# First expert on inputs without their norm in every block, and the second expert's weight words converted in place

## The chip, the cores and the metric

One core of a Trainium2 chip. The metric is the device time of one execution, in microseconds (us). TensorE does the matrix products, VectorE, ScalarE and GpSimd (POOL in the rows) the elementwise work, SyncE issues the DMAs.

## The reference

Attention of 4 batches, 8 heads, 576 positions, head size 64: heads 0 to 3 see the last 32 positions, heads 4 to 7 every 32nd position. Its output, 2304 tokens by 512, goes through two experts in series, each 512 to 1536 to 512:

```python
x = attention(q, k, v)                                    # 2304 x 512
xn = x / sqrt(mean(x * x, axis=-1) + 1e-6) * rms_g
x2 = (silu(xn @ w_gate) * (xn @ w_val)) @ w_out           # expert 1
out = (x2 @ w_a * (x2 @ w_b)) @ w_out2                    # expert 2
```

The norm of a token is one factor for its whole row. So `xn @ w` is `(x * rms_g) @ w` times that factor, and the value product's factor may be put on expert 1's output.

## The kernel before

**Tiling.** The tokens are cut into 6 blocks of 384 (96 positions of each of the 4 batches; columns of a tile), d_ff into 12 slots of 128. Expert 1 runs block after block: per slot 12 matmuls of the gate product (`g_ps`), 12 of the value product (`v_ps`) and 12 of the output `y` of the slot before. Each product is three matmuls of split numbers (high by high, high by low, low by high, `mm3`, L474 to L477), so its input `xx` is a pair: a high half, cast on ScalarE, and a low half, the difference, on VectorE or GpSimd. `h = sg * v_ps` (L747) is split in the same way into `hl` (L489 cast on ScalarE, L490 difference).

**PSUM.** `g_ps` and `v_ps` take turns in three banks, so a bank is used again 36 matmuls after its product is complete; `y` has four banks, and one bank, `att`, is left to the attention.

**Attention beside it.** While block t goes through the expert, the attention of block t+1 is put into its slots (`attention_slot`, L600; the string table `LOCAL`, L51 to L54, says which step stands in which slot). Local heads run on TensorE with softmax on VectorE and ScalarE (`s_t`, L298 to L332). Strided heads are products on GpSimd (`prod`, L232 and L265) and sums on VectorE (`S_t` L235, `xs_t` L268), 57 of each. Every instruction's place on its engine is then set by a scheduler, so the order on an engine differs from the order of the code.

**The norm before.** Blocks 1 to 5: the attention's output is copied out of PSUM (`x_t`, L381 and L397, ScalarE), squared (`sq`) and summed with one matmul (`rms`), the square root goes to ScalarE and the reciprocal to VectorE (`rinv`, L427). Then `xprep` (L430) makes for each of the 4 channel tiles `xn = x_t * g * rinv` on VectorE (L433), the high half `xx` (L437, ScalarE) and the low half (L438: VectorE for blocks 2 and 4, GpSimd for 1, 3 and 5, by the string `XLO`). These steps stand in slot 11 of the block before, and the block's first matmul needs the first of them. Block 0 does it in another way: `xx` is made from the output times `g` alone, each gate product is multiplied by the reciprocal `ri0` on VectorE (L736) ahead of Silu (L737), and so is each of the four `y` (L588).

**Outputs.** The four `y` of a block are taken out of PSUM in slot 1 of the next block (`evac_y`: `ys` on ScalarE, L590, for blocks 1 to 5) and written to DRAM (`x2d`).

**Block 5.** It has no attention beside it. Instead the second expert's weights are turned into seven sums per group, the forms (`convert_forms`, L622): a raw tile (`raw`, 2 buffers, load L106), its words (`words`: a Prelu on ScalarE, L129, writes the tile `cy`, one buffer; a second ScalarE pass, L134, writes `z0` or `z1`, one buffer each; VectorE puts the two together in `z`, L137), casts on ScalarE (L142), differences (L143) and sums (`zs`, L656 to L659, on GpSimd where the group's number is odd, else on VectorE). Also `slab` tiles of block 0's and 1's output are loaded and subtracted (L693). Loads stand in SyncE's one queue in order. From 593.7 us on only the second expert runs.

## Time and profile before

| | |
|---|---|
| median of 3 runs | 1018.35 us (1016.94 to 1019.04) |
| the profiled execution | 1017.75 us, its span 1016.0 us |
| mean granted clock of TensorE | 0.973 |
| first gate matmul of blocks 1 to 5 | 141.5, 228.8, 317.2, 406.1, 501.9 us |
| expert 1 ends | 593.7 us |

Times in the rows are microseconds from the span's start, means are nanoseconds. A busy time counts instructions in work, not in wait. In the waits, the line left of the arrow waited and the one at its right came last. The granted clock of a stretch is a mean: 1.00 is 2.4 GHz, and a part of it at 1.2 GHz counts one half.

### The profile page before, as it was taken

The numbers are of one execution on the slowest core, as the hardware profiler recorded it, in microseconds if no ns is written. First come the engines' busy times: TensorE is split into PE (matmuls) and PEld (weight loads), VectorE is DVE, ScalarE is ACT, GpSimd is POOL, SyncE is SP. The second block draws the span as 40 slices with busy tenths as digits, with TensorE's granted clock in tenths as the row PEclk, the third lists the DMA queues.
The fourth block names the chain that finished last, engine by engine and source line by source line (L and its number), as shares of the span: only waits on it lengthen the run. The fifth ranks groups of instructions, "written<-read, shape, count | busy, mean of one in ns | idle before, by whom it ended". The sixth has DMA issues, their size and how long they took to land.

```text
span 1016.0 us, 14355 instructions
## 1 busy us (share of the span) xinstructions
PE 961.8 (95%) x5438; PEld 908.7 (89%) x5438; DVE 640.6 (63%) x869; ACT 427.5 (42%) x832; POOL 543.2 (53%) x416
## 2 busy tenths in 40 slices
PE   6898799999999999699959999999999999999998
PEld 5698699998998999599959999999999998999996
DVE  5699957538808674978366536866856556455444
ACT  4878645236223523342366552644533432222110
POOL 4588747456729776678365722656651533223111
PEclk6999999999999999899989999999999999999999
DMA  9953357435534453242299946599894783772701
GB/s 349 407 208 122 107 188 279 130 115 171 165 113 151 154 173 122 88 142 81 90 341 367 372 156 252 197 392 394 311 376 190 286 301 136 272 308 105 271 40 63
DMA packets 57365, 215.57 MB, mean 212 GB/s; under 512 B 5968, under 2 KB 14544, under 8 KB 51664
## 3 DMA queue, kind: packets, MB, share of 16 engines
q1 hardware_dynamic: 57296, 214.66, 58.0%
q8 instruction: 43, 0.70, 0.3%
q14 instruction: 26, 0.21, 0.1%
HBM read 172.17 MB, written 42.47 MB: 211 GB/s over the span
## 4 chain that ended last, share of the span: by engine, by line
PE 69%; DVE 13%; ACT 6%; POOL 4%; issue 4%; DMA 3%; SPq 0%; DVEq 0%; POOLq 0%; ACTq 0%
PE o L878 4%; PE o L880 4%; PE o L879 4%; PE Y L822 3%; PE Y L824 3%; PE Y L823 3%; PE g_ps L476 3%; PE v_ps L475 3%; PE v_ps L476 3%; PE g_ps L475 3%; PE y L476 3%; PE v_ps L477 3%; PE g_ps L477 3%; PE y L475 3%; PE y L477 3%
## 5 line engine op out<-in xcount | busy, mean ns | idle before, releaser
L143 POOL TENSOR_TENSOR hl<-c,hl 128x384 fp32r<-128x384 f32 x72 | 77.4, 1076 | 190.8 <-ACT hl L142 180.2
L232 POOL TENSOR_TENSOR prod<-kv_t,qs_t 128x512 f32<-128x512 f32 (+12 forms) x57 | 106.8, 1894 | 18.9 <-DVE S_t L235 6.1
L475 PE MATMUL g_ps<-xx,gv 128*128 128x384 f32 x288 | 100.6, 349 | 12.7 <-DVE h L747 11.4
L490 POOL TENSOR_TENSOR hl<-h,hl 128x384 fp32r<-128x384 f32 x58 | 63.6, 1096 | 79.4 <-ACT hl L489 78.0
L475 PE MATMUL v_ps<-xx,gv 128*128 128x384 f32 x288 | 98.6, 343 | 7.2 <-ACT sg L737 4.8
L476 PE MATMUL g_ps<-xx,gv 128*128 128x384 f32 x288 | 100.4, 349 | 4.9 <-DVE xx L438 4.9
L477 PE MATMUL g_ps<-xx,gv 128*128 128x384 f32 x288 | 99.6, 346 | 0.0
L477 PE MATMUL y<-hl,wo 128*128 128x384 f32 x288 | 99.0, 344 | 0.0
L829 DVE TENSOR_TENSOR c<-c,Y 128x384 f32<-128x384 f32 x108 | 59.1, 551 | 63.2 <-PE Y L824 57.8
L476 PE MATMUL y<-hl,wo 128*128 128x384 f32 x288 | 98.3, 341 | 0.3 <-DVE hl L490 0.2
L265 POOL TENSOR_TENSOR prod<-kv_t,S_t 128x512 f32<-128x512 f32 (+12 forms) x57 | 85.4, 1511 | 23.8 <-issue 7.8
L476 PE MATMUL v_ps<-xx,gv 128*128 128x384 f32 x288 | 98.0, 340 | 0.0
L477 PE MATMUL v_ps<-xx,gv 128*128 128x384 f32 x288 | 97.6, 339 | 0.0
L268 DVE TENSOR_REDUCE xs_t<-prod 128x64 f32<-128x448 f32 (+17 forms) x57 | 85.4, 1517 | 13.2 <-POOL prod L265 13.0
L747 DVE TENSOR_TENSOR h<-sg,v_ps 128x384 f32<-128x384 f32 x72 | 39.0, 542 | 80.7 <-PE v_ps L477 62.3
L475 PE MATMUL y<-hl,wo 128*128 128x384 f32 x288 | 85.4, 344 | 0.6 <-ACT hl L489 0.6
L878 PE MATMUL o<-slab,hl 128*128 128x512 f32 x216 | 84.6, 392 | 1.0 <-DVE slab L887 0.5
L879 PE MATMUL o<-slab,hl 128*128 128x512 f32 x216 | 84.6, 392 | 0.0
L880 PE MATMUL o<-slab,hl 128*128 128x512 f32 x216 | 83.4, 394 | 0.0
L142 ACT CAST hl<-c 128x384 fp32r<-128x384 f32 x72 | 36.9, 513 | 109.5 <-DVE c L859 109.3
L822 PE MATMUL Y<-slab,form 128*128 128x384 f32 x216 | 73.1, 338 | 0.1
L824 PE MATMUL Y<-slab,form 128*128 128x384 f32 x216 | 73.1, 338 | 0.0
(142 smaller groups left out, 2546.5 us busy)
## 6 DMA issues: line engine op xcount, KB each, us to landing
form<-formd SPq DMA_DIRECT2D x32, 1792.0 KB, 10.6
wo<-wod SPq DMA_DIRECT2D x60, 512.0 KB, 3.7
raw<-in_w SPq DMA_DIRECT2D x42, 512.0 KB, 5.5
gv_raw<-in_w SPq DMA_DIRECT2D x30, 512.0 KB, 10.1
formd<-form SPq DMA_DIRECT2D x6, 1792.0 KB, 9.1
formd<-forms SPq DMA_DIRECT2D x6, 1792.0 KB, 11.1
slab<-x2d SPq DMA_DIRECT2D x24, 384.0 KB, 5.8
wod<-wo SPq DMA_DIRECT2D x12, 512.0 KB, 2.9
```

The costliest lines, as they stand in the source:

```text
L143: lo_eng.tensor_tensor(lo, x, hi.bitcast(F32), op=ALU.subtract)
L232: nc.gpsimd.tensor_tensor(pr, st["ks", g][:, :, :n, :], st["qs"][:, heads(g), mm:mm + 1, :].to_broadcast([128, G, n, D]), op=ALU.mult)
L265: st["pvm"] = nc.gpsimd.tensor_tensor(pr, st["vs", g][:, :, :n, :], st["S"][:, heads(g), mm, :n, None].to_broadcast([128, G, n, D]), op=AL ...
L268: st["pvr"] = nc.vector.tensor_reduce(st["xs"][:, mm, heads(g), :], pr.rearrange("p g n d -> p g d n"), axis=X, op=ALU.add)
L475: nc.tensor.matmul(out_ps, w_hi, x_hi, start=start, stop=False)
L476: nc.tensor.matmul(out_ps, w_hi, x_lo, start=False, stop=False)
L477: nc.tensor.matmul(out_ps, w_lo, x_hi, start=False, stop=stop)
L822: nc.tensor.matmul(bank(n), hi, x[p][:, 0, c], start=begins and c == 0, stop=False, skip_group_check=not begins)
L824: nc.tensor.matmul(bank(n), lo, x[p][:, 0, c], start=False, stop=c == 1, skip_group_check=not begins)
L878: nc.tensor.matmul(o, h[:, 0, cols], w[0], start=n == 0, stop=False)
L879: nc.tensor.matmul(o, h[:, 0, cols], w[1], start=False, stop=False)
L880: nc.tensor.matmul(o, h[:, 1, cols], w[0], start=False, stop=n == len(chunks) - 1)
```

## The change

Blocks 1 to 5 are done as block 0. As soon as an attention output stands in PSUM, `xsplit` takes it out times `g` (`x_t`, ScalarE), squares it from PSUM, and makes both halves of `xx` (the low one on the engine that `XLO` says). `xprep` with its 20 `xn` on VectorE is gone. All 60 gate products of blocks 1 to 5 are multiplied by `ri[t]` on VectorE, Silu then reads that tile, and the 20 `ys` of blocks 1 to 5 go from ScalarE's copies to VectorE's products. The forms' words have no `cy` any more: Prelu writes into the odd words of the raw tile itself, so the raw tile is in use until VectorE has put the words together. The same holds for the second expert's output weights (the last part of the diff). Instructions: VectorE 871 before, 931 after; ScalarE 782 and 764; TensorE, GpSimd and SyncE keep their numbers.

```diff
-          "lnorm0 lvl0 pt0 ptc0 lnorm1 lvl1|pt1 ptc1 lnorm2 pt2 ptc2||pv0 pvc0 pv1 pvc1 sq0|sq1|"),
+          "lnorm0 lvl0 pt0 ptc0 lnorm1 lvl1|pt1 ptc1 lnorm2 pt2 ptc2||pv0 pvc0 pv1 pvc1||"),
...
-          "lnorm0 lexp1 lvl1 pt0 ptc0 lnorm1 lnorm2|pt1 pt2 ptc1||ptc2 pv0 pvc0 pv1 pvc1 sq0 sq1||")]
+          "lnorm0 lexp1 lvl1 pt0 ptc0 lnorm1 lnorm2|pt1 pt2 ptc1||ptc2 pv0 pvc0 pv1 pvc1||")]
...
-            st["y"] = pool.tile([128, DM], F32, tag="cy", name="cy", bufs=ncy)
+            st["y"] = pool.tile([128, DM], F32, tag="cy", name="cy", bufs=ncy) if ncy else raw[:, :, 1].bitcast(F32)
...
+        def xsplit(i, src):
+            x_t = piece("xr", "x_t", 4)
+            nc.scalar.activation(x_t, src, AF.Copy, scale=g_sb[:, i:i + 1])
+            sq(i)()
+            xx = xt[t, i] = act.tile([128, 2, NTB], F32R, tag="x", name="xx", bufs=8)
+            nc.scalar.copy(xx[:, 0], x_t)
+            engine(XLO[t]).tensor_tensor(xx[:, 1], x_t, xx[:, 0].bitcast(F32), op=ALU.subtract)
...
-                x_t = st["x", p] = piece("xr", "x_t", 4)
-                nc.scalar.copy(x_t, st["ops", p][:, :NTB])
+                xsplit(p, st["ops", p][:, :NTB])
...
-                src = st["ops" if i < 2 else "xps", i % 2][:, :NTB] if t == 0 else st["x", i]
+                src = st["ops" if i < 2 else "xps", i % 2][:, :NTB]
...
-        def xprep(cc):
-            def f():
-                xn = act.tile([128, NTB], F32, tag="t", name="xn", bufs=NTMP)
-                nc.vector.scalar_tensor_tensor(
-                    xn, st["x", cc],
-                    g_sb[:, cc:cc + 1], st["ri"], op0=ALU.mult, op1=ALU.mult)
-                xx = act.tile([128, 2, NTB], F32R, tag="x", name="xx", bufs=8)
-                nc.scalar.copy(xx[:, 0], xn)
-                engine(XLO[t]).tensor_tensor(xx[:, 1], xn, xx[:, 0].bitcast(F32), op=ALU.subtract)
-                xt[t, cc] = xx
-            return f
+            ri[t] = act.tile([128, NTB], F32, tag="ri", name="rinv", bufs=2)
+            st["rec"] = nc.vector.reciprocal(ri[t], r)
...
-            if t == 0:
-                nc.vector.tensor_tensor(ys, y[t, e][:, :NTB], ri0, op=ALU.mult)
-            else:
-                nc.scalar.copy(ys, y[t, e][:, :NTB])
+            nc.vector.tensor_tensor(ys, y[t, e][:, :NTB], ri[t], op=ALU.mult)
...
-            st["words", i] = words(st["raw", i], z(i), pool, 1)
+            st["words", i] = words(st["raw", i], z(i), pool, 0)
...
-            if t == 0:
-                nc.vector.tensor_tensor(sg, g_ps[:, :NTB], ri0, op=ALU.mult)
-            nc.scalar.activation(sg, sg if t == 0 else g_ps[:, :NTB], AF.Silu)
+            nc.vector.tensor_tensor(sg, g_ps[:, :NTB], ri[t], op=ALU.mult)
+            nc.scalar.activation(sg, sg, AF.Silu)
```

The first place is VectorE at the end of block 3 and the start of block 4 (the names carry the number of their tile; `h_3964` is the last but one product of block 3). Before:

```order
L235 TENSOR_REDUCE S_t_4066<-prod_4072 128x16
L427 RECIPROCAL rinv_3948<-rms_t_3946 128x384
L747 TENSOR_TENSOR h_3964<-sg_3942,v_ps_3929 128x384
L235 TENSOR_REDUCE S_t_4066<-prod_4134 128x17
L235 TENSOR_REDUCE S_t_4066<-prod_4137 128x18
L433 SCALAR_TENSOR_TENSOR xn_3997<-x_t_3758,cst_sb_113,rinv_3948 128x384
L433 SCALAR_TENSOR_TENSOR xn_4002<-x_t_3769,cst_sb_113,rinv_3948 128x384
L433 SCALAR_TENSOR_TENSOR xn_4007<-x_t_3883,cst_sb_113,rinv_3948 128x384
L298 SCALAR_TENSOR_TENSOR s_t_4225<-att_4149,cst_sb_113 128x384
L438 TENSOR_TENSOR xx_3999<-xn_3997,xx_3999 128x384
L438 TENSOR_TENSOR xx_4004<-xn_4002,xx_4004 128x384
L235 TENSOR_REDUCE S_t_4066<-prod_4142 128x16
```

The same place in the change, where `sg_4018` belongs to block 3's last slot:

```order
L723 TENSOR_TENSOR sg_3832<-g_ps_3806,rinv_3123 128x384
L385 TENSOR_TENSOR xx_3784<-x_t_3779,xx_3784 128x384
L734 TENSOR_TENSOR h_3861<-sg_3832,v_ps_3819 128x384
L723 TENSOR_TENSOR sg_3892<-g_ps_3866,rinv_3123 128x384
L734 TENSOR_TENSOR h_3933<-sg_3892,v_ps_3879 128x384
L385 TENSOR_TENSOR xx_3904<-x_t_3899,xx_3904 128x384
L723 TENSOR_TENSOR sg_3964<-g_ps_3938,rinv_3123 128x384
L385 TENSOR_TENSOR xx_3916<-x_t_3911,xx_3916 128x384
L237 TENSOR_REDUCE S_t_4071<-prod_4077 128x16
L734 TENSOR_TENSOR h_3987<-sg_3964,v_ps_3951 128x384
L723 TENSOR_TENSOR sg_4018<-g_ps_3992,rinv_3123 128x384
L436 RECIPROCAL rinv_3971<-rms_t_3969 128x384
```

The three `xn` and the `xx` behind the reciprocal are gone from the block's boundary; the low halves `xx` stand ahead of the reciprocal, between the `sg` and `h` of block 3's last slots.

The second place is VectorE in block 5, from the second group of forms on (`h_5025` is the product of slot 1, `z0_5191` a word of the third group, `slab` the loads for the second expert). Before:

```order
L137 SCALAR_TENSOR_TENSOR z0_5063<-cy_5061,z0_5063 128x512
L137 SCALAR_TENSOR_TENSOR z1_5067<-cy_5065,z1_5067 128x512
L143 TENSOR_TENSOR slab_5056<-slab_4911,slab_5056 128x768
L693 TENSOR_TENSOR slab_4911<-slab_4911 128x768
L693 TENSOR_TENSOR slab_4911<-slab_4971,slab_4911 128x768
L137 SCALAR_TENSOR_TENSOR z0_5191<-cy_5189,z0_5191 128x512
L747 TENSOR_TENSOR h_5025<-sg_4993,v_ps_4958 128x384
L747 TENSOR_TENSOR h_5088<-sg_5072,v_ps_5043 128x384
```

The same place in the change, from the four `ys` of block 4 on (`h_5033` is the product of slot 1):

```order
L578 TENSOR_TENSOR ys_5003<-y0_4160,rinv_3971 128x384
L578 TENSOR_TENSOR ys_5006<-y1_4161,rinv_3971 128x384
L578 TENSOR_TENSOR ys_5009<-y2_4162,rinv_3971 128x384
L578 TENSOR_TENSOR ys_5012<-y3_4163,rinv_3971 128x384
L138 SCALAR_TENSOR_TENSOR z0_5198<-raw_5193,z0_5198 128x512
L144 TENSOR_TENSOR slab_5064<-slab_4919,slab_5064 128x768
L681 TENSOR_TENSOR slab_4919<-slab_4919 128x768
L734 TENSOR_TENSOR h_5033<-sg_5000,v_ps_4965 128x384
L723 TENSOR_TENSOR sg_5078<-g_ps_5038,rinv_4819 128x384
```

The `z0` of the third group still stands ahead of slot 1's `h`, and the four `ys` have come in ahead of it. On SyncE the fifth load of a raw tile now stands ahead of the four stores of those `ys`; before it stood behind them.

## Rows read from the trace of the kernel before

**Rows 1.** The page, part 1: busy us, share of the span, instructions.

```profile
PE 961.8 (95%) x5438; PEld 908.7 (89%) x5438; DVE 640.6 (63%) x869; ACT 427.5 (42%) x832; POOL 543.2 (53%) x416
```

**Rows 2.** Busy time of each engine by stretch; the first line names the columns.

```profile
core 0: us, PE busy (x) PEld busy (x) DVE busy (x) ACT busy (x) POOL busy (x), PEclk, DMA share, GB/s
100.00:141.50 41.50, 33.41 (x193) 30.66 (x191) 36.25 (x38) 25.43 (x45) 24.44 (x18) 0.92 0.37 127
228.80:317.20 88.40, 85.95 (x538) 82.66 (x537) 52.96 (x67) 35.61 (x78) 55.33 (x42) 1.00 0.44 146
317.20:406.10 88.90, 86.65 (x537) 83.96 (x536) 60.31 (x69) 33.99 (x58) 66.86 (x44) 0.98 0.48 154
406.10:436.00 29.90, 21.80 (x111) 19.50 (x110) 29.07 (x33) 9.85 (x17) 19.95 (x10) 0.89 0.31 101
501.90:541.30 39.40, 28.99 (x153) 27.94 (x152) 23.34 (x28) 22.09 (x43) 24.76 (x23) 0.87 0.88 315
541.30:593.70 52.40, 52.17 (x301) 51.85 (x300) 28.19 (x34) 29.81 (x56) 30.99 (x26) 1.00 0.87 330
593.70:1016.00 422.30, 417.24 (x2162) 387.45 (x2161) 245.84 (x379) 139.91 (x256) 157.59 (x132) 1.00 0.63 240
```

**Rows 3.** TensorE's waits, 100 to 141.5: us in total, times, longest.

```profile
PE att L388 <- DVE xs_t L268: 2.1, 1, 2.1
PE att L388 <- ACT x_t L381: 1.5, 1, 1.5
...
PE g_ps L475 <- ACT xx L437: 1.3, 1, 1.3
```

**Rows 4.** TensorE's waits, block 2 (228.8 to 317.2).

```profile
PE g_ps L476 <- DVE xx L438: 1.4, 2, 1.0
```

**Rows 5.** TensorE's waits, block 3 (317.2 to 406.1).

```profile
PE att L280 <- DVE s_t L298: 2.2, 1, 2.2
```

**Rows 6.** TensorE's waits, block 4's start (406.1 to 436).

```profile
PE g_ps L476 <- DVE xx L438: 3.5, 2, 2.3
PE v_ps L475 <- ACT sg L737: 3.1, 1, 3.1
```

**Rows 7.** Timeline of VectorE, 403 to 432: start us, us, instruction.

```profile
408.03 2.84 DVE L438 TENSOR_TENSOR xx<-xn,xx 128x384 fp32r<-128x384 f32 x2
...
412.39 2.73 DVE L438 TENSOR_TENSOR xx<-xn,xx 128x384 fp32r<-128x384 f32 x1
415.04 0.60 DVE L433 SCALAR_TENSOR_TENSOR xn<-x_t,cst_sb,rinv 128x384 f32<-128x384 f32 x1
...
418.16 2.73 DVE L438 TENSOR_TENSOR xx<-xn,xx 128x384 fp32r<-128x384 f32 x1
```

**Rows 8.** VectorE by line: busy us, mean ns | idle before, releasers.

```profile
L747 DVE TENSOR_TENSOR h<-sg,v_ps 128x384 f32<-128x384 f32 x72 | 39.0, 542 | 80.7 <-PE v_ps L477 62.3 <-issue 12.9 <-ACT sg L737 3.0
...
L433 DVE SCALAR_TENSOR_TENSOR xn<-x_t,cst_sb,rinv 128x384 f32<-128x384 f32 x20 | 21.6, 1110 | 4.5 <-POOL hl L490 3.4 <-POOL xx L438 1.1
...
L736 DVE TENSOR_TENSOR sg<-g_ps,ri 128x384 f32<-128x384 f32 x12 | 6.6, 548 | 0.0
```

**Rows 9.** ScalarE by line and shape, the same columns.

```profile
L737 ACT ACTIVATE sg<-g_ps 128x384 f32<-128x384 f32 x60 | 29.1, 490 | 60.9 <-PE g_ps L477 57.4 <-issue 2.3 <-POOL prod L265 0.6
...
L737 ACT ACTIVATE sg<-sg 128x384 f32<-128x384 f32 x12 | 6.3, 523 | 3.2 <-DVE sg L736 3.1
```

**Rows 10.** TensorE's waits, block 5's start (501.9 to 541.3).

```profile
PE g_ps L475 <- DVE h L747: 9.1, 1, 9.1
```

**Rows 11.** Timeline of ScalarE and VectorE inside that wait.

```profile
526.89 0.83 ACT L142 CAST form<-zs 128x768 fp32r<-128x768 f32 x1 [0.99 <-POOL zs L659]
527.63 0.66 ACT L134 ACTIVATE z<-raw 128x512 uint32<-128x512 uint16 x1
...
528.39 2.18 DVE L137 SCALAR_TENSOR_TENSOR z<-cy,z 128x512 uint32<-128x512 uint32 x1 [0.72 <-ACT z L134]
```

**Rows 12.** SyncE's queue, 495 to 520: what a DMA issue waited for.

```profile
SPq L106 <- DVE xn L433: 7.8, 1, 7.8
```

More of the change, by code (lines that the diff above doesn't have):

```diff
@@ L169, in fused_kernel @@
     xt = {}
+    ri = {}
     def attention(t, pool, psum, banks):
@@ L395, in f @@
                     return xhl(2 + p, st["xps", p][:, :NTB])
-                x_t = st["x", 2 + p] = piece("xr", "x_t", 4)
-                nc.scalar.copy(x_t, st["xps", p][:, :NTB])
+                xsplit(2 + p, st["xps", p][:, :NTB])
             return f
@@ L425, in rinv @@
             st["sqrt"] = nc.scalar.activation(r, st["rps"][:, :NTB], AF.Sqrt, bias=eps_sb[:, 0:1])
-            ri = ri0 if t == 0 else act.tile([128, NTB], F32, tag="t", name="rinv", bufs=NTMP)
-            st["rec"] = nc.vector.reciprocal(ri, r)
-            st["ri"] = ri
-        def xprep(cc):
-            def f():
-                xn = act.tile([128, NTB], F32, tag="t", name="xn", bufs=NTMP)
-                nc.vector.scalar_tensor_tensor(
-                    xn, st["x", cc],
-                    g_sb[:, cc:cc + 1], st["ri"], op0=ALU.mult, op1=ALU.mult)
-                xx = act.tile([128, 2, NTB], F32R, tag="x", name="xx", bufs=8)
-                nc.scalar.copy(xx[:, 0], xn)
-                engine(XLO[t]).tensor_tensor(xx[:, 1], xn, xx[:, 0].bitcast(F32), op=ALU.subtract)
-                xt[t, cc] = xx
-            return f
+            ri[t] = act.tile([128, NTB], F32, tag="ri", name="rinv", bufs=2)
+            st["rec"] = nc.vector.reciprocal(ri[t], r)
         for hf in range(2):
@@ L450, in attention @@
                 steps[f"{name}{g}"] = f(g)
-        for i in range(4):
-            steps[f"sq{i}"] = sq(i)
         steps["lq"] = load_q
@@ L461, in attention @@
         steps["rms"], steps["rinv"], steps["st"], steps["sqrt_set"] = rms, rinv, st, sqrt_set
-        for cc in range(NCC):
-            steps[f"xp{cc}"] = xprep(cc)
         ng = 4 // G
@@ L469, in attention @@
                 lst.insert(max(0, 3 * (g - 1)), f"{ld}{g}")
-        steps["strided"] = ["lq"] + qk_steps + ["ssub", "sexp", "snorm"] + pv_steps + ["xst0", "xstc0", "xst1", "xstc1", "sq2", "sq3"]
+        steps["strided"] = ["lq"] + qk_steps + ["ssub", "sexp", "snorm"] + pv_steps + ["xst0", "xstc0", "xst1", "xstc1"]
         return steps
@@ L505, in fused_kernel @@
     ones = const1.tile([128, 128], F32, name="ones")
-    ri0 = const1.tile([128, NTB], F32, name="ri0")
     apool = ExitStack()
@@ L604, in attention_slot @@
         part += local[min(t, 1)].get(fc, "").split()
-        part += ["rms", "rinv"] * (fc == n_sl) + [f"xp{cc}" for cc in range(4)] * (fc == n_sl + 1)
+        part += ["rms", "rinv"] * (fc == n_sl)
         for n in part:
@@ L785, in begin @@
         def begin():
-            st["words"] = words(st["raw"], z, pool, 1)
+            st["words"] = words(st["raw"], z, pool, 0)
             st["words"][0]()
```

## Prediction

> **What bounds the kernel now.** I read the busy shares first, then the stretches, then TensorE's waits inside the stretches that are short of full, then the timeline of the engine those waits name. TensorE is busy 961.8 of a span of 1016.0 us [rows 1], so only its idle time and its half-clocked time can be won; the matmuls themselves do not change in number. The stretches show where that is [rows 2]. The second expert (593.7 to the end) leaves 422.30 − 417.24 = 5.1 us at clock 1.00, and the end of block 5 leaves 0.2: nothing to win there. What is open lies at the seams of expert 1: 41.50 − 33.41 = 8.1 us at the end of block 0, 2.5 in block 2, 2.3 in block 3, 8.1 at the start of block 4, 10.4 at the start of block 5. The granted clock adds to it: 0.92, 0.98, 0.89 and 0.87 in four of these, that is (1 − 0.89) × 29.9 = 3.3 us at block 4's start, and likewise 3.3, 1.8 and 5.1 in the other three; the fall to the lower level (1.2 GHz) stands in the stretches in which TensorE waited. All numbers are set against the profiled execution, 1017.75 us; the median of the runs is 0.6 above it.
>
> **The cost, part by part.**
>
> *End of block 0.* TensorE waited 2.1 and 1.5 us for the attention of block 1 and 1.3 for the first `xx` [rows 3]. The last goes whole: `xx` is now made from the attention output without the reciprocal, so it is ready before block 1 starts. Of the other two (3.6), VectorE's and ScalarE's later work is relieved by the missing `xn` and casts, but the one attention bank is held longer, since Square now reads PSUM too (about one pass, 490 ns as Silu's [rows 9]); I take half, 1.8. Together **3.1**. Ends: −1.0 (two Squares on the path) and 8.1 + 3.3 = 11.4.
>
> *Block 2.* The wait for the low half of `xx`, 1.4 [rows 4], goes: **1.4**, ends −0.5 (one `sg` late) and 2.5.
>
> *Block 3.* Here the wait is for a masked score on VectorE, 2.2 [rows 5], which stands behind that engine's queue of reduces. VectorE is busy 60.31 of 88.90. The change puts 12 `sg` there and takes nothing from this wait by itself, but the four `xn` and the low halves of the block's start are no longer bunched at one seam. I take the 2.2 and half of the 1.8 that the clock lost, **3** rounded; ends 0 and 4.1. Below nothing is the first rival.
>
> *Start of block 4.* VectorE is busy 29.07 of 29.90 us, so it is what TensorE waits for: 3.5 us for low halves and 3.1 for a slot that came late behind them [rows 6]. The change removes four low halves and one `xn` from this stretch, with the durations that they had there: 2.84 + 2.73 + 2.73 + 0.60 = 8.9 us [rows 7]; the other three `xn` stood ahead of it. It adds four `sg` (four slots at most start in it) and four `ys`. The nearest row for both is block 0's own `sg`, 548 ns [rows 8]: 8 × 0.548 = 4.4. VectorE is relieved by **4.5**, and since it is full, TensorE gets that. I leave the clock's 3.3 out of the sum; ends 0 and 8.1 + 3.3 = 11.4.
>
> On the price of the products from PSUM: ScalarE took the same tile in 490 ns [rows 9] and VectorE takes it in 548. The Trainium skill (VectorE: DVE Perf Modes, the table at its head) speaks against this move: VectorE lies closer to SBUF and ScalarE to PSUM. The rows agree in the sign, by 58 ns; over the 80 moved or added products that would be 4.6 us of VectorE's time if all lay on the path, and none does where VectorE has room.
>
> *The other seams' low halves.* They are not removed, they move into slots 7 to 10 of the block before, between `sg` and `h` (the order of VectorE at block 3's end). GpSimd is busy 66.86 of block 3's 88.90 us, and an `xx` beside it took 2.73 where an unhindered difference of that shape would take about an `h`'s 542 ns [rows 2, 7, 8]. The Trainium skill (SBUF — State Buffer, Who interferes with whom) says that a VectorE instruction with two SBUF inputs contends with GpSimd's reads; by that rule the moved low halves keep their 2.73 in the new place and only the seam is freed, while if they fell to 542 ns VectorE would be relieved by 2.2 us more for each. The sum does not count on the latter.
>
> *The 60 `sg`.* In other slots they cost nothing on the path while this cover holds: a bank is asked for again 36 matmuls after its product is complete. At 52.17 / 301 = 0.173 us each [rows 2] that is 6.2 us, against 0.55 for `sg` and at worst a low half ahead of it (2.73). Silu, 523 ns from SBUF [rows 9], is needed by `h`; the 12 matmuls of the value product (2.1 us) cover 0.55 + 0.52 = 1.1. The cover is gone where VectorE's queue ahead of an `sg` is longer than 6.2 − 0.55 = 5.7 us; then each further us is one on the path. ScalarE loses 20 copies and is at 42%: nothing either way.
>
> *Block 5.* TensorE waits 9.1 us once, for `h` of slot 1 [rows 10]. That `h` stands on VectorE behind the third group's `z` (2.18), which waits for ScalarE's second word pass, which stands behind the cast of the sums made on GpSimd [rows 11]. The change's order keeps this chain and puts the four `ys` (2.2 us) ahead of a `z` that waits for ScalarE in any case. What moves the chain: the raw loads no longer wait 7.8 us for the last `xn` [rows 12], but each raw tile is now held until VectorE has joined the words, 2.28 us later in this place (530.57 against 528.29, from [rows 11]), and three loads follow one another on two buffers. TensorE itself comes about 5 us earlier by the part above, so it would meet the chain sooner. I take a gain of **2**; ends −3 (the three loads late by 2.28 each would be 6.8, of which TensorE's earlier arrival and the 7.8 us give back more than half) and the whole of it, 9.1 + 5.1 of the clock = 14.2.
>
> *In place words, second expert.* 5.1 us of idle time in 422.30, with raw loads that come far ahead: 0.
>
> Sum: 3.1 + 1.4 + 3 + 4.5 + 2 = 14.0, so 1003.75 in the profiled execution and, 0.6 above it, **1004.4** as a median. With the ends that are likely together it spans 996 to 1010.
>
> **The rivals.**
>
> *VectorE becomes the bound (slower).* Blocks 3 and 4 are where VectorE has least room. If the `sg` there do not find a gap, Silu, `h` and the banks come late: 24 `sg` × 0.548 = 13.2 and 8 `ys` × 0.548 = 4.4 come on the path, and the gains of block 3 and block 4 are not made. That gives 1017.75 + 17.6 − (3.1 + 1.4 + 2) = 1028.9, as a median 1029.5. For it: 29.07 of 29.90 at block 4's start. Against it: 60.31 of 88.90 over block 3, and 6.2 us of cover for each. It decides once VectorE's queue ahead of an `sg` passes 5.7 us slot after slot.
>
> *The forms' stall goes too (faster).* If the earlier raw loads pull the chain wholly ahead of slot 1's `h`, the remaining 7.1 of the 9.1 go and the clock's 5.1 of block 5 with them: 14.0 + 7.1 + 5.1 = 26.2, so 992.2 (985 to 996 with what the clock does at block 0 and 4). For it: the 7.8 us of SyncE's wait. Against it: the order keeps `z0` ahead of `h`, and its chain through GpSimd's sums.
>
> *The gains are given back.* If block 4's start only swaps its low halves for `sg` and `ys` that wait behind reduces, blocks 3 and 4 give nothing, and the longer hold of the raw tiles costs the 3 us of the end above: 3.1 + 1.4 − 3 = 1.5, so 1016.9, 1014 to 1019. For it: the low halves of [rows 7] move to a place with as much GpSimd work. Against it: there they have slots of time.
>
> **How the numbers follow.** Forecast 53%, the forms' stall gone too 24%, gains given back 13%, VectorE the bound 10%. A measurement of this kernel tells about 0.2% from no change, 2 us. Faster by more: 53 + 24 + 5 of the 13 = 0.82; within: 0.06; slower: 10 + 2 = 0.12. For 8 in 10 the range takes the forecast's 996 to 1010, most of the second (from 987) and half of the third (to 1016); it leaves out the 10 of the slow case and some 8 at its ends.
>
> **What would show it.** Right: no wait of `g_ps` for `xx` in any block; at block 4's start VectorE some 25 of 30 us busy and TensorE idle by less than 4; one wait of 6 to 9 us for `h` in block 5, still behind `z`; `sg` near 550 ns also beside GpSimd's products. Wrong: `sg` waits on VectorE above 1 us in blocks 2 to 4 (first rival); no such wait in block 5 (second); raw loads that come later than before and a longer wait for `h` (third). The forecast falls if the time is above 1016 or below 987.

## The result, and the profile after

The changed kernel takes 988.55 us (988.09 to 989.53, 4 runs) against 1017.64 us (1016.05 to 1019.04) of the kernel before: the ratio is 0.9716 with a 95% interval of 0.9698 to 0.9733, a gain of 29.1 us where 14.0 was forecast. The time lies in the stated range and on its side; the size of the change is off by a little more than a factor of two. The profiled execution took 988.63 us, its span 986.9 us, mean granted clock 0.979.

The page's part 1 of the changed kernel, beside [rows 1]:

```profile
PE 950.1 (96%) x5438; PEld 902.5 (91%) x5438; DVE 651.8 (66%) x929; ACT 422.5 (43%) x814; POOL 540.4 (55%) x416
```

TensorE's busy time fell by 11.7 us and its idle time by 17.4 (54.2 before, 36.8 now). VectorE's rose by 11.2. The stretches that answer to [rows 2] (end of block 0; blocks 2 and 3; block 4's start; block 5's start; the second expert; same columns):

```profile
97.00:137.20 40.20, 34.28 (x204) 31.78 (x204) 35.26 (x38) 27.85 (x50) 30.46 (x23) 0.96 0.33 112
223.90:307.50 83.60, 83.60 (x530) 81.87 (x530) 51.03 (x75) 35.09 (x76) 56.34 (x45) 1.00 0.47 154
307.50:391.90 84.40, 84.40 (x537) 82.67 (x537) 66.97 (x85) 31.58 (x53) 62.31 (x40) 1.00 0.48 161
391.90:421.80 29.90, 29.90 (x189) 29.58 (x188) 27.35 (x39) 13.59 (x18) 29.90 (x16) 1.00 0.49 156
477.40:516.90 39.50, 32.89 (x181) 32.57 (x181) 28.99 (x39) 23.07 (x43) 20.26 (x19) 0.91 0.88 332
565.10:986.90 421.80, 416.32 (x2161) 386.99 (x2159) 245.77 (x383) 138.75 (x254) 161.40 (x133) 1.00 0.63 241
```

Blocks 2 and 3 and the start of block 4 have no idle time at all and clock 1.00; block 4's start had 8.1 us idle and 0.89. VectorE is still busy for 27.35 of the 29.90 us there (29.07 before). At block 5's start 6.6 us are still idle. TensorE's waits of the changed kernel, over the whole run:

```profile
PE g_ps L467 <- DVE h L734: 7.8, 2, 6.6
PE att L398 <- DVE xs_t L270: 5.2, 2, 3.3
...
PE v_ps L467 <- DVE sg L723: 2.4, 1, 2.4
```

No wait for `xx` is left, 6.6 of the 7.8 us for `h` are block 5's, and none of the three lines is a wait in blocks 2 or 3 or at block 4's start. VectorE by line and shape, beside [rows 8]:

```profile
L723 DVE TENSOR_TENSOR sg<-g_ps,rinv 128x384 f32<-128x384 f32 x72 | 39.4, 547 | 39.5 <-PE g_ps L469 39.0 <-DMA x2d<-ys 0.4
...
L578 DVE TENSOR_TENSOR ys<-y,rinv 128x384 f32<-128x384 f32 x24 | 11.7, 544 | 1.4 <-PE y L469 1.4
...
L385 DVE TENSOR_TENSOR xx<-x_t,xx 128x384 fp32r<-128x384 f32 x8 | 6.7, 840 | 12.5 <-ACT xx L384 12.5
```

The new products cost 547 and 544 ns, as taken from block 0's. The low halves, moved, fell from 1699 ns (mean of 8 before) to 840.

One table carries most of what follows: the length of each block, from its first gate matmul to the next block's (block 5: to the start of expert 1's last output matmul), read from each kernel's timeline of TensorE, in us. Each row is one profiled execution. A seam is the end of one block and the start of the next; a wait ahead of a block's first gate matmul counts to the block before it.

| kernel | block 0 | 1 | 2 | 3 | 4 | 5 | rest |
|---|---|---|---|---|---|---|---|
| before | 106.7 | 87.3 | 88.4 | 89.0 | 95.7 | 91.9 | 422.3 |
| the change | 103.3 | 86.7 | 83.6 | 84.4 | 85.5 | 87.4 | 422.0 |
| words_only | 105.8 | 87.3 | 88.5 | 87.9 | 95.8 | 89.6 | 423.8 |
| before_low_halves_on_gpsimd | 105.7 | 87.2 | 88.2 | 88.0 | 94.4 | 92.8 | 421.7 |
| before_vector_takes_psum | 106.1 | 89.0 | 88.9 | 90.3 | 98.9 | 83.0 | 421.7 |
| xn_early_before | 110.7 | 85.2 | 84.2 | 84.4 | 85.0 | 86.6 | 421.7 |
| xn_on_gpsimd_before | 107.4 | 87.0 | 89.1 | 92.5 | 89.1 | 81.6 | 423.5 |
| idle_xn | 103.6 | 85.8 | 88.2 | 88.9 | 91.5 | 82.3 | 422.7 |
| wait_for_reciprocal | 104.4 | 88.9 | 87.8 | 86.1 | 88.6 | 82.2 | 422.4 |
| both_put_back | 106.4 | 97.0 | 97.2 | 103.8 | 90.9 | 85.8 | 421.9 |
| halves_after_reciprocal | 102.0 | 86.0 | 84.7 | 84.4 | 88.7 | 86.4 | 422.0 |
| outputs_in_own_buffers | 102.2 | 86.7 | 83.6 | 84.4 | 85.4 | 79.9 | 421.9 |

Of the 29.1 us, blocks 2, 3 and 4 gave 4.8, 4.6 and 10.2, block 5 gave 4.5, blocks 0 and 1 gave 4.0; about 1 came ahead of the first gate matmul, where nothing was changed. In the five runs below that edit the changed kernel's block 5 alone, blocks 2 to 4 repeat the change's within 0.1 us, blocks 0 and 1 within 1.5.

### The profile page after: what moved, and what is told of

Its sections match the earlier page's. It is cut to its first block, busy times and chain, and to the rows that moved or that the text cites. A ratio compares the mean times of both kernels' runs of the same rounds, so it can differ in the third digit from the quotient of the medians.

```text
span 986.9 us, 14413 instructions
## 1 busy us (share of the span) xinstructions
PE 950.1 (96%) x5438; PEld 902.5 (91%) x5438; DVE 651.8 (66%) x929; ACT 422.5 (43%) x814; POOL 540.4 (55%) x416
## 4 chain that ended last, share of the span: by engine, by line
PE 69%; DVE 5%; DMA 3%; POOL 3%; issue 2%; ACT 2%; SPq 0%; DVEq 0%; ACTq 0%; POOLq 0%
PE o L865 5%; PE o L867 5%; PE o L866 5%; PE Y L811 4%; PE Y L809 4%; PE Y L810 4%; PE y L467 3%; PE v_ps L467 3%; PE y L468 3%; PE g_ps L467 3%; PE y L469 3%; PE v_ps L469 3%; PE g_ps L469 3%; PE g_ps L468 3%; PE v_ps L468 3%; PE X L809 2%
## 5 line engine op out<-in xcount | busy, mean ns | idle before, releaser
L467 PE MATMUL g_ps<-xx,gv 128*128 128x384 f32 x288 | 98.9, 343 | 7.8 <-DVE h L734 7.8
L267 POOL TENSOR_TENSOR prod<-kv_t,S_t 128x512 f32<-128x512 f32 (+12 forms) x57 | 85.2, 1508 | 26.8 <-DVE xs_t L270 9.2
L469 PE MATMUL g_ps<-xx,gv 128*128 128x384 f32 x288 | 97.8, 340 | 0.0
L468 PE MATMUL y<-hl,wo 128*128 128x384 f32 x288 | 97.6, 339 | 0.1
L468 PE MATMUL g_ps<-xx,gv 128*128 128x384 f32 x288 | 97.7, 339 | 0.0
L469 PE MATMUL y<-hl,wo 128*128 128x384 f32 x288 | 96.7, 336 | 0.0
L467 PE MATMUL y<-hl,wo 128*128 128x384 f32 x288 | 85.6, 345 | 1.3 <-ACT hl L481 1.3
L865 PE MATMUL o<-slab,hl 128*128 128x512 f32 x216 | 84.7, 393 | 1.6 <-DVE slab L874 1.2
L724 ACT ACTIVATE sg<-sg 128x384 f32<-128x384 f32 x72 | 37.8, 525 | 92.8 <-DVE sg L723 86.9
## 6 DMA issues: line engine op xcount, KB each, us to landing
gv_raw<-in_w SPq DMA_DIRECT2D x30, 512.0 KB, 10.2
```

Source lines behind the costliest of these rows:

```text
L267: st["pvm"] = nc.gpsimd.tensor_tensor(pr, st["vs", g][:, :, :n, :], st["S"][:, heads(g), mm, :n, None].to_broadcast([128, G, n, D]), op=AL ...
L467: nc.tensor.matmul(out_ps, w_hi, x_hi, start=start, stop=False)
L468: nc.tensor.matmul(out_ps, w_hi, x_lo, start=False, stop=False)
L469: nc.tensor.matmul(out_ps, w_lo, x_hi, start=False, stop=stop)
L865: nc.tensor.matmul(o, h[:, 0, cols], w[0], start=n == 0, stop=False)
```

## The experiments

**Parts of the change done alone.** First the words in place, and the low halves of blocks 2 and 4 on GpSimd, each on the kernel before:

```diff
-            st["words", i] = words(st["raw", i], z(i), pool, 1)
+            st["words", i] = words(st["raw", i], z(i), pool, 0)
```

> The kernel before with the words converted in place and nothing else of the change; the norm stays on the inputs. Two theories of the changed kernel's 29 us. Seam: the inputs of a block no longer hang on the reciprocal, and everything in blocks 1 to 5 follows from that; then this run is within 2 us of before (1015.6 to 1019.6), with block 5's wait for h still about 9 us. Words: the 4.4 us that block 5 gained (91.9 to 87.5 us) come from the in-place words; then this run is faster by 3 to 5 us and the wait for h is 7 us or less. Third possibility, from the raw tiles being held longer: slower by 1 to 3 us.

Measured: 1015.66 us, ratio 0.998 (0.9964 to 0.9995). The gain is 1.6 us (0.5 to 3.7 by the interval). In the profiled execution it lies in block 5 (89.6 for 91.9, with a wait for `h` of 7.7 us for 9.1), and 1.5 are given back behind it.

```diff
-XLO = "DPDPDP"
+XLO = "DPPPPP"
```

> The kernel before with the low halves of blocks 2 and 4 on GpSimd instead of VectorE, as blocks 1, 3 and 5 have them. If the seams of blocks 2 and 4 were dear because the low halves stood in VectorE's full queue, this alone gives 4 to 9 us (1009 to 1014), most of it in block 4. If they were dear because all of xx hangs on the reciprocal and on xn, it gives less than 2 us, or loses, since GpSimd then stands between the products and the block's start.

Measured: 1015.2 us, ratio 0.9983 (0.9968 to 0.9998). The engine of the low halves alone was not the matter: block 4 still takes 94.4.

**Halves behind the reciprocal again.** On the changed kernel, casts and differences are written behind `with tc.issue_after(st["rec"].ins)` in slot 11:

> The changed kernel, with the high and low halves of xx in blocks 1 to 5 made only after the reciprocal of their block, as xn was before; no xn is made, and gate products and outputs are multiplied as in the change. Seam theory: the wait of the block's first matmuls for xx comes back and VectorE has the four low halves of block 4 at the block's start again; the time goes back by 8 to 16 us, to 997 to 1005, most of it in blocks 2 and 4. Rival, less work: the gain came from the 21.6 us of xn that VectorE no longer does and from cheaper low halves; then it stays within 3 us of the change (987 to 991).

Measured: 991.84 us, ratio 0.9742 (0.9717 to 0.9767); 3.3 us back, so the seam theory seemed to fall. It did not, because the edit did less than its text says: in this run the construct held back VectorE's instructions alone. ScalarE's timeline in this run has the casts where the change has them,

```profile
379.35 0.53 ACT L390 CAST xx<-x_t 128x384 fp32r<-128x384 f32 x1
...
384.21 0.51 ACT L390 CAST xx<-x_t 128x384 fp32r<-128x384 f32 x1
```

and VectorE's has the reciprocal after them, with the four low halves behind it:

```profile
391.26 2.54 DVE L443 RECIPROCAL rinv<-rms_t 128x384 f32<-128x384 f32 x1
393.72 3.16 DVE L391 TENSOR_TENSOR xx<-x_t,xx 128x384 fp32r<-128x384 f32 x4
```

Only VectorE's low halves of blocks 2 and 4 were held back, 3.16 us for four in block 4, which became 3.2 us longer.

**The price of the new products.** Each `sg` of blocks 1 to 5 written twice:

```diff
-            nc.vector.tensor_tensor(sg, g_ps[:, :NTB], ri[t], op=ALU.mult)
+            for _ in range(1 if t == 0 else 2):
+                nc.vector.tensor_tensor(sg, g_ps[:, :NTB], ri[t], op=ALU.mult)
```

> The changed kernel with every gate product of blocks 1 to 5 multiplied twice on VectorE (the same result written two times), 60 more instructions of 0.55 us, 33 us in all. Cover theory: a bank is asked for again only 36 matmuls (6.2 us) later, so next to nothing reaches TensorE: 988 to 993. Rival, VectorE close to being the bound in blocks 3 and 4: 24 of them (13 us) reach the path, 999 to 1004, with waits of TensorE for sg or h in these blocks.

Measured: 990.92 us, ratio 0.9731 (0.9707 to 0.9755). 33 us more on VectorE cost 2.4, and the interval overlaps the change's: the cover of 36 matmuls holds, and VectorE is not the bound by its load.

**Who takes the products out of PSUM.** A theory formed then, that ScalarE had held the banks too long, was tried from both sides. On the kernel before (with the words in place), VectorE takes `g_ps` and `y` out times a tile of ones:

```diff
-                nc.scalar.copy(ys, y[t, e][:, :NTB])
+                nc.vector.tensor_tensor(ys, y[t, e][:, :NTB], unit, op=ALU.mult)
...
+            nc.vector.tensor_tensor(sg, g_ps[:, :NTB], ri0 if t == 0 else unit, op=ALU.mult)
+            nc.scalar.activation(sg, sg, AF.Silu)
```

> The kernel before with the norm still on its inputs (reciprocal, xn, halves at the block's boundary), words in place, and one thing of the change without its purpose: in blocks 1 to 5 VectorE takes every gate product (60) and every output (20) out of PSUM, times a tile of ones, and Silu reads that tile. Bank theory, formed on the run with the halves after the reciprocal: before, a gate product's bank was given back by Silu, which stood in ScalarE's order behind exponentials of the attention (the Silus of slots 0 and 1 of block 4 ran together at 427.5, after an exponential that had waited for VectorE); now VectorE gives it back. Then this run, though it adds 44 us to VectorE's work, is faster than before by 10 us or more: 1000 to 1007. Rival, the xn: what counted was the 21.6 us of xn on VectorE between the reciprocal and the block; then nothing is gained, 1014 to 1020, or lost with VectorE's 44 us, up to 1030.

And on the changed kernel the products are left out, and with them the norm of blocks 1 to 5; ScalarE reads PSUM as before:

```diff
-            nc.vector.tensor_tensor(sg, g_ps[:, :NTB], ri[t], op=ALU.mult)
-            nc.scalar.activation(sg, sg, AF.Silu)
+            nc.scalar.activation(sg, g_ps[:, :NTB], AF.Silu)
```

> The changed kernel without the norm's products in blocks 1 to 5 (this run leaves the norm of these blocks out): Silu reads the gate product from PSUM on ScalarE and ScalarE copies the outputs, as before; 80 VectorE instructions, 44 us, are gone, and the halves are made early as in the change. Bank theory: 10 us or more of the gain are lost, 999 to 1006, with TensorE waiting for ScalarE's sg at the starts of blocks 2 to 4 again. Rival, the xn: it keeps the whole gain and perhaps some us more from the lighter VectorE, 984 to 989.

Measured: 1017.21 us, ratio 0.9987 (0.9973 to 1.0001), and 989.34 us, ratio 0.9716 (0.9693 to 0.9739). The bank theory fell twice over: the first gains nothing, the second loses nothing. In the first, blocks 1 to 4 are 7.6 us longer in sum than with the words alone while block 5 is 6.6 shorter, which the total alone would have hidden.

**Work and dependence put back, one at a time and together.** On the changed kernel, `idle_xn` puts the 20 `xn` back behind each reciprocal with no reader; `wait_for_reciprocal` makes the halves wait by data instead:

```diff
+                xn = act.tile([128, NTB], F32, tag="t", name="xn", bufs=NTMP)
+                nc.vector.scalar_tensor_tensor(xn, st["x", cc], g_sb[:, cc:cc + 1], ri[t], op0=ALU.mult, op1=ALU.mult)
```

```diff
+                with tc.issue_after(st["rec"].ins):
+                    nc.vector.tensor_scalar(x_t[:, 0:1], x_t[:, 0:1], 1.0, None, op0=ALU.mult)
                 xx = xt[t, i] = act.tile([128, 2, NTB], F32R, tag="x", name="xx", bufs=8)
                 nc.scalar.copy(xx[:, 0], x_t)
```

> The changed kernel with the 20 xn of before put back on VectorE behind each reciprocal as idle work: nothing reads them, the halves of xx stay early. It adds 21.6 us of VectorE's time at the blocks' ends and no wait for TensorE by data. Work theory (VectorE's time at the seam was the loss): 20 us or more come back, 1005 to 1015. Dependence theory (a block's first matmuls hung on the reciprocal through xn, cast and difference, and all that VectorE and ScalarE did at the seam stood in between): at most 5 come back, 988 to 993.5.

> The changed kernel with the dependence put back without the work: behind each reciprocal VectorE writes one column of each x_t (times one), and the casts and differences of xx come after that, so the block's first matmul again hangs on the reciprocal through VectorE, ScalarE and the low half's engine; no xn. Dependence theory: 12 to 25 us come back, 1000 to 1014, with waits for xx at the start of every block. Work theory: 6 or less, 988 to 995.

> The two put back together: idle xn behind the reciprocal, and the halves after xn and after a one-column write. If the two theories share the 29 us, this run returns nearly all of it: 1010 to 1020, more than either alone. If neither is the cause it stays below 1000.

Measured: 997.07 (ratio 0.9777, 0.9749 to 0.9805), 996.64 (0.9783, 0.976 to 0.9806) and 1037.95 us (1.019, 1.0166 to 1.0213): 8.5, 8.1 and 49.4 us above the change. Neither alone is what either theory expected of itself. The blocks say more than the totals. Idle `xn` makes blocks 2, 3 and 4 longer by 4.6, 4.5 and 6.0 us, 15.1 of the 19.6 that these blocks had gained, though nobody reads them; the total hides it, since block 5 became 5.1 shorter. VectorE's `xn` behind the reciprocals at the starts of blocks 2, 3 and 4 in that run,

```profile
228.53 4.27 DVE L442 SCALAR_TENSOR_TENSOR xn<-x_t,cst_sb,rinv 128x384 f32<-128x384 f32 x4
...
316.66 4.95 DVE L442 SCALAR_TENSOR_TENSOR xn<-x_t,cst_sb,rinv 128x384 f32<-128x384 f32 x4
...
406.37 5.72 DVE L442 SCALAR_TENSOR_TENSOR xn<-x_t,cst_sb,rinv 128x384 f32<-128x384 f32 x4
```

and block 4's start, with the wait that grew there:

```profile
401.50:431.40 29.90, 26.13 (x149) 25.81 (x148) 29.61 (x33) 9.30 (x14) 25.13 (x13) 0.94 0.42 138
```

```profile
PE g_ps L476 <- DVE h L743: 3.8, 1, 3.8
```

The four `xn` stand ahead of an `h`, and a bank is given back only when that `h` has read it. At these three seams VectorE's queue is full, and what is put into it comes out about one for one (4.27, 4.95 and 5.72 us put in, 4.6, 4.5 and 6.0 lost). Only a part of the loss carries the name of `h`: 2.8, 2.2 and 3.8 us. The granted clock of the first 30 us of each of these blocks is 0.94 instead of the 1.00 of the change, which is some 1.8 us more. At the starts of blocks 1 and 5, where the four `xn` took 2.4 us, the blocks did not become longer.

The dependence alone makes blocks 2 to 4 longer by 9.0 us in sum. With both, TensorE waits for both kinds of things:

```profile
PE g_ps L484 <- ACT xx L392: 11.9, 3, 4.9
PE v_ps L484 <- DVE sg L740: 9.5, 4, 2.9
PE g_ps L484 <- DVE h L751: 8.4, 3, 4.3
```

The 49.4 us are three times the sum of the two totals, but they are not the price of what the change removed: that was 29.1, and `before_vector_takes_psum`, which has `xn`, the dependence and the products on VectorE as well, took 1017.21. The edit put back more than there had been. At block 4 all four `xn` (VectorE) now stand ahead of the first cast (ScalarE), which starts 11.5 us behind the reciprocal's start (425.64):

```profile
430.96 5.18 DVE L450 SCALAR_TENSOR_TENSOR xn<-x_t,cst_sb,rinv 128x384 f32<-128x384 f32 x4
```

```profile
437.17 0.51 ACT L392 CAST xx<-x_t 128x384 fp32r<-128x384 f32 x1 [9.53 <-DVE x_t L390]
```

In the kernel before, the first cast follows the first `xn`, 6.0 us behind the reciprocal's start (397.75):

```profile
403.72 0.51 ACT L437 CAST xx<-xn 128x384 fp32r<-128x384 f32 x1 [0.55 <-DVE xn L433]
```

At blocks 2 and 3 it is 10.0 and 9.4 us against 5.3 and 4.5. No run has the two together in the order of the kernel before, so how much of the 49.4 us this order makes is not shown.

**The same two from the side of the kernel before.** First all of the work is left and only its place is changed: `xn`, casts and differences stand where each output is copied out (no norm in blocks 1 to 5: `xn` is the larger of `x * g` and `x`):

```diff
-                    g_sb[:, cc:cc + 1], st["ri"], op0=ALU.mult, op1=ALU.mult)
+                    g_sb[:, cc:cc + 1], st["x", cc], op0=ALU.mult, op1=ALU.max)
...
-        part += ["rms", "rinv"] * (fc == n_sl) + [f"xp{cc}" for cc in range(4)] * (fc == n_sl + 1)
+        part += ["rms", "rinv"] * (fc == n_sl)
```

> The kernel before with its 20 xn, casts and low halves made as soon as each attention output is copied out, not behind the reciprocal (the norm of blocks 1 to 5 is left out: xn is the larger of x times g and x, by an instruction of the same form with the same two SBUF inputs). VectorE and ScalarE have the same instructions as before; only their place and what they hang on differ. If the dependence with VectorE's work on it is the loss, most of the gain comes from this alone: 990 to 1000. If VectorE's time is the loss wherever it lies: 1010 to 1019.

Measured: 994.3 us, ratio 0.977 (0.9748 to 0.9792): 23.3 us gained with the same instructions. Blocks 2, 3 and 4 take 84.2, 84.4 and 85.0, as in the change; block 0 is 4.0 longer than before, so the earlier place is not free everywhere. VectorE by line, and the low halves of the kernel before behind it:

```profile
L433 DVE SCALAR_TENSOR_TENSOR xn<-x_t,cst_sb 128x384 f32<-128x384 f32 x20 | 14.3, 716 | 36.5 <-ACT x_t L381 27.1 <-ACT x_t L397 9.4
...
L438 DVE TENSOR_TENSOR xx<-xn,xx 128x384 fp32r<-128x384 f32 x8 | 5.3, 661 | 6.5 <-ACT xx L437 6.5
```

```profile
L438 DVE TENSOR_TENSOR xx<-xn,xx 128x384 fp32r<-128x384 f32 x8 | 13.4, 1699 | 0.0
```

In the new place `xn` takes 716 ns instead of 1110 and a low half 661 instead of 1699. Then the dependence is left and `xn` goes to GpSimd:

```diff
-                nc.vector.scalar_tensor_tensor(
-                    xn, st["x", cc],
-                    g_sb[:, cc:cc + 1], st["ri"], op0=ALU.mult, op1=ALU.mult)
+                nc.gpsimd.tensor_tensor(xn, st["x", cc], st["ri"], op=ALU.mult)
```

> The kernel before with xn made on GpSimd (x_t is scaled by g as it is copied out of PSUM), still behind the reciprocal and ahead of the halves. The dependence stays, its longest piece of VectorE's work is gone, and GpSimd has 20 instructions of some 1.1 us more among its products. If what counts is that xn stands in VectorE's full queue: 998 to 1008. If the dependence is dear by whatever engine it runs through: 1012 to 1022.

Measured: 1007.01 us, ratio 0.9892 (0.9873 to 0.9911). The total fits the first case, its blocks do not: 2 and 3 became longer (89.1, 92.5), block 4 shorter by 6.6, and 10.3 of the gain lie in block 5, whose wait for `h` is gone in this run. GpSimd now stands in the chain: at block 3 it makes the first two `xn` at 315.2 and 316.2 and, behind its products and low halves, the other two at 325.0 and 325.9.

**Block 5's wait.** Four edits on the changed kernel. Holding each slot's share of the conversion behind `h` of two slots before; the second group's sums on VectorE; one `z` behind `h` of slot 1; that and the slab work:

```diff
-                run(early[len(early) * fc // NFC:len(early) * (fc + 1) // NFC])
+                with tc.issue_after(h_ins[fc - 2]) if fc >= 2 else nullcontext():
+                    run(early[len(early) * fc // NFC:len(early) * (fc + 1) // NFC])
```

> The changed kernel with each slot's share of block 5's conversion held back until h of two slots before has been issued, so that no z of the third group can stand ahead of slot 1's h on VectorE. If the 6.6 us wait and the clock it costs (0.09 of 39.5 us, 3.6) are that order alone: 979 to 985. If the forms, started later, are then late for the second expert: 987 to 995, with new waits behind 565 us.

> The changed kernel with the four sums of the second group of forms on VectorE instead of GpSimd; the order of z ahead of slot 1's h stays. If the chain through GpSimd's sums and ScalarE's cast is what makes z late, the wait of 6.6 us falls to 3 or less: 983 to 986. If the raw load or ScalarE is late in any case: within 2 us of the change.

> The changed kernel with one instruction moved: the third group's first z on VectorE in block 5 is put behind h of slot 1 (before, it stood ahead of it and made TensorE wait 6.6 us). If that order alone makes the wait: the 6.6 us and up to 3.6 us of clock go, 978.5 to 983. If another word or the loads behind it take its place as what h or TensorE waits for: 984 to 989. The run that held back whole shares of the conversion removed the wait in block 5 but lost as much in the second expert; this one leaves the other forms where they were.

> The changed kernel with slot 1's h in block 5 ahead of both the third group's z and the slab work of the first x forms on VectorE (and slot 4's ahead of those of slot 5). If the order on VectorE is all that makes TensorE wait there, the 5 to 6.6 us and up to 3.6 us of clock go: 978 to 984. If h then waits for a buffer held by the stores of ys (DMA, 1.1 us in the run with one word moved) or the work moved comes late for the second expert: 984 to 988.

Measured: 990.92 (ratio 0.9728, 0.9702 to 0.9754), 988.54 (0.9716, 0.969 to 0.9743), 987.41 (0.9692, 0.9672 to 0.9712) and 988.11 us (0.9714, 0.9688 to 0.9739). None is told apart from the change by its interval. Block 5's wait for `h`, 6.6 us in the change, was 1.7, 6.0, 5.4 and 5.1 us. The first edit lost its gain again behind block 5: the rest took 425.9 us for 422.0, and what made it longer was not followed. In the third, the next VectorE instruction in line took the place of `z`, and behind it `h` had a releaser that no forecast had named:

```profile
498.14 1.38 DVE L144 TENSOR_TENSOR slab<-slab 128x768 fp32r<-128x768 f32 x1 [5.36 <-ACT slab L143]
...
501.62 0.56 DVE L742 TENSOR_TENSOR h<-sg,v_ps 128x384 f32<-128x384 f32 x1 [1.10 <-DMA x2d<-ys]
```

In the fourth, with all of that out of the way, the same `h` waited for it alone:

```profile
497.50 0.55 DVE L743 TENSOR_TENSOR h<-sg,v_ps 128x384 f32<-128x384 f32 x1 [8.64 <-DMA x2d<-ys]
```

It is a store of `ys`. `h`, `sg` and `ys` take turns in five buffers (`NTMP`), and three of the four stores stood in SyncE's queue behind two slab loads:

```profile
488.57 2.54 SPq L674 DMA_DIRECT2D slab<-x2d  x2
491.20 2.96 SPq L579 DMA_DIRECT2D x2d<-ys  x3
```

So the four `ys` of block 4 went into buffers of `xx`, of which four are free by then:

```diff
-            ys = tmp("ys")
+            ys = tmp("ys") if t != NB - 2 else act.tile([128, 2, NTB], F32, tag="x", name="ys", bufs=8)[:, 0]
```

> The changed kernel with the four ys of block 4 in buffers of xx that are free by then, instead of the five that sg, h and ys share. If h of slot 1 in block 5 waited for a buffer that a store of ys still held, the 6.6 us and up to 3.6 us of clock go: 978 to 983, and no wait above 2 us is left between 477 us and the end of block 5. If the chain of words (raw load, ScalarE, z) is the cause whatever the buffers: within 2 us of the change.

Measured: 981.08 us (979.77 to 981.39), ratio to before 0.964 (0.9623 to 0.9657), faster than both kernels: 7.5 us less than the change, and the two ranges do not touch. The same stretch at block 5's start is full:

```profile
477.80:517.30 39.50, 39.49 (x228) 39.17 (x228) 31.42 (x44) 24.58 (x46) 19.89 (x19) 1.00 0.91 352
```

With no buffer to wait for, the scheduler itself put `h` of slot 1 ahead of the third group's `z`,

```profile
493.24 0.56 DVE L734 TENSOR_TENSOR h<-sg,v_ps 128x384 f32<-128x384 f32 x1 [0.59 <-ACT sg L724]
...
497.93 1.81 DVE L138 SCALAR_TENSOR_TENSOR z<-raw,z 128x512 uint32<-128x512 uint32 x1 [2.53 <-ACT z L135]
```

so the order on VectorE, in which the forecast saw the cause, goes with the buffers in the changed kernel. The wait, with the 3.6 us that the clock of 0.91 cost in those 39.5 us, was worth 10, and 7.5 of it came back.

> The same for the ys of all six blocks. If only block 5 suffers from the shared buffers (its stores wait in SyncE's queue behind raw and slab loads), no more than 1 us beyond the run with block 4's alone. If the seams of blocks 2 to 4 suffer too, 1 to 3 us more.

Measured: 985.13 us, ratio 0.9682 (0.9665 to 0.9698): 4 us more than with block 4's alone, which neither expectation had. In the profiled execution block 1 takes 89.1 us for 86.7 and block 2 84.3 for 83.6; why they lose by it was not followed.

## Why the prediction was right in sign and wrong in size

- **Where the open time lay**: right. The gain came at the seams of expert 1, and the second expert (422.3 and 422.0 us) gave nothing.
- **End of block 0**, 3.1: measured 3.4 in block 0, which differs by up to 1.5 us between the runs that edit block 5 alone. The wait of 1.3 for `xx` is gone. The waits for the attention's bank fell by 1.3 (6.4 to 5.1 us in four places; the forecast counted two of them, 3.6, and took half), and Square, which reads that bank now, shows up among them:

```profile
PE att L364 <- ACT sq L418: 2.6, 1, 2.6
```

- **Block 2**, 1.4: measured 4.8. **Block 3**, 3: measured 4.6. **Block 4**, 4.5: measured 10.2. These three are the terms that were mis-sized, by 10.7 us of the 15 that are missing. The step that failed is the way they were sized: for blocks 2 and 3 by the waits that name `xx` or a score [rows 4, 5], for block 4 by what VectorE loses and gains inside one stretch, where "the other three `xn` stood ahead of it" counted nothing and the clock's 3.3 was left out. In their place nearly all that TensorE had open there came back: in block 3 2.3 idle and 1.8 of clock, 4.1 against 4.6 measured; at block 4's start 8.1 and 3.3, 11.4 against 10.2; block 2 gave 4.8, more than its 2.5 idle, and TensorE's busy time there fell too, from 85.95 to 83.60. VectorE's load inside block 4's start fell by 1.7 us only, where 4.5 had been forecast. What was relieved is its queue, and a full queue carries over a boundary. VectorE's timeline of the kernel before has those three `xn` just ahead of block 4:

```profile
403.08 4.56 DVE L433 SCALAR_TENSOR_TENSOR xn<-x_t,cst_sb,rinv 128x384 f32<-128x384 f32 x3
```

With them, the relief by the forecast's own sum is 8.9 + 4.56 − 4.4 = 9.1, against 10.2 measured. `idle_xn` shows such a price directly: four `xn` of 4.27, 4.95 and 5.72 us, put back at a seam with no reader, cost 4.6, 4.5 and 6.0 us in blocks 2 to 4. VectorE now goes from the reciprocal to block 4's own work at once:

```profile
391.89 2.54 DVE L436 RECIPROCAL rinv<-rms_t 128x384 f32<-128x384 f32 x1
394.36 1.23 DVE L237 TENSOR_REDUCE S_t<-prod 128x17 f32<-128x1088 f32 x1
395.50 0.54 DVE L734 TENSOR_TENSOR h<-sg,v_ps 128x384 f32<-128x384 f32 x1
...
397.22 0.55 DVE L723 TENSOR_TENSOR sg<-g_ps,rinv 128x384 f32<-128x384 f32 x1
```

- **What was removed was of less account than where it stood.** The forecast for block 4 listed removals and additions; `xn_early_before` keeps all of VectorE's work and gains 23.3 us, with blocks 2 to 4 as short as in the change. The dependence on the reciprocal is what held the work at the seam; put back by itself it cost 4.2, 1.7 and 3.1 us in these blocks.
- **The low halves keep their 2.73 us in the new place**: wrong. They take 840 ns in the change and 661 in `xn_early_before`. The Trainium skill (SBUF — State Buffer, Who interferes with whom) ties the slow case to GpSimd's reads at the same time. The traces agree. In the kernel before, six of the eight low halves on VectorE began while GpSimd made a product, and each ended 0.4 us after that product did; the other two met no GpSimd instruction and took 0.55 us. The product beside the low half of 412.39 [rows 7] ends at 414.70, the low half at 415.12:

```profile
412.08 2.62 POOL L232 TENSOR_TENSOR prod<-kv_t,qs_t 128x1152 f32<-128x1152 f32 x1 [2.09 <-DVE S_t L235]
```

In the change a low half meets a sum of squares of 1.01 us instead, or nothing (0.54 to 0.56 us). Here GpSimd's sum ends at 373.70, VectorE's low half at 374.12:

```profile
372.69 1.01 POOL L424 TENSOR_TENSOR sq<-sq 128x384 f32<-128x384 f32 x1 [3.75 <-ACT sq L418]
```

```profile
373.05 1.07 DVE L385 TENSOR_TENSOR xx<-x_t,xx 128x384 fp32r<-128x384 f32 x1 [1.90 <-ACT xx L384]
```

GpSimd's share of busy time in the block, from which the forecast argued, did not tell what it does at that moment.
- **The products on VectorE**: right in price (547 and 544 ns against 548) and in cover. That ScalarE lies closer to PSUM (the Trainium skill, VectorE: DVE Perf Modes, Specifications) is in line with the 58 ns, which lie between two different instructions, and mattered nothing: the interval of `change_scalar_takes_psum` overlaps the change's.
- **Block 5**, 2: measured 4.5, with 6.6 of the 9.1 us of wait left. Of the 4.5, `words_only` has 2.3; the rest was not traced. The chain named (sums, cast, `z`) was not what bound it in the changed kernel: there ScalarE waited for the raw load ahead of that `z`,

```profile
494.46 0.66 ACT L130 ACTIVATE raw<-raw 128x512 f32<-128x512 f32 x1 [3.74 <-DMA raw<-in_w]
```

sums on VectorE left the wait at 6.0 us, and the buffers of `ys` freed 7.5 us. Whether the same buffers made the 9.1 us before was not tried; there the last of the four stores had been issued by 523.0, 7.5 us ahead of that `h` (530.50).
- **The rivals.** VectorE as the bound: fell as stated, since 33 us more cost 2.4; but `both_put_back`, at 1037.95, shows its sign, waits for `sg` of up to 2.9 us, where the dependence is kept. The forms' stall gone too: its time, 992.2, was nearest to the result, its mechanism did not occur. That the result lies inside the stated range is therefore luck: the range reached down to 987 for this rival's sake. The gains given back: fell, since blocks 2 to 4 gave 19.6 us, though a raw load did come late in block 5.

## What to carry to other kernels

Size the relief of a full in-order engine by everything that it no longer does from the moment its queue fills, across the boundary of the stretch, and by the clock that comes back, and not by the waits that carry a name alone: those are the end of the queue only. Work that a late value holds at a seam where that queue is full cost about its own length here; the same work earlier left blocks 2 to 4 as short as without it and cost 4 us in block 0. So break the dependence first. And judge an edit by stages as well as by the total: in four of these runs block 5 became five to ten us shorter, which hid what happened in the blocks in question.

## What the runs showed that had not been expected

A wait that the order of an engine seemed to explain belonged to a shared buffer, held by a store in another queue: the row showed it (8.64 us released by `x2d<-ys`) only after the instructions ahead were gone. The low half of an input, the same instruction on the same shape, took between 0.54 and 2.73 us in the kernel before and in the change, and what GpSimd was doing at that moment set it: where a GpSimd instruction was under way, the low half ended 0.4 us after it. And an edit that puts two parts of a change back can put back more than both: with all four `xn` ahead of the first cast it cost 49.4 us, 20 more than the whole change had gained.
